# Gated mix of attention and a gated linear unit: alternating periods, value sums copied by ACT, maxima turned by DVE

## The chip, the cores and the metric

The kernel runs on one NeuronCore of a Trainium2 chip. The metric is the device time of one execution in microseconds (us). PE is the matmul engine TensorE (PEld its weight loads), DVE the vector engine VectorE, ACT the scalar engine ScalarE, POOL GpSimd, and SP the engine whose queue issues nearly all DMAs. PE writes its results to PSUM, which has eight banks of 128 x 512 f32.

## The reference

```python
S, D, H, Dh, F = 2048, 512, 32, 16, 1792
g = sigmoid((x * gate_w).sum(-1, keepdims=True))
q, k, v = split(x @ wqkv)                       # 32 heads of 16
a = softmax(q k^T / sqrt(Dh)) v  @ wo           # per head over 2048 keys
b = (sigmoid(x @ w_gate) * (x @ w_up)) @ w_down
return g * a + (1 - g) * b
```

## The kernel before, in words

All matmuls but those of the values take operands that are split into a high and a low part (`split`), so that a product becomes three. Attention goes over 16 pairs of heads. The first head of a pair lies in partitions 0 to 63 (the lower half of PE), the second in 64 to 127 (the upper half): matmuls of the two halves run beside each other on PE if they are issued next to each other.

For each head the row maxima of the scores are found first (`sm_step`: a 128 x 512 score matmul, L250, and a DVE reduce, L252). The maxima of eight query tiles (half of a head's rows, called a half here) are gathered in `stat`, reduced to one row (L256), turned by a PE transpose (`put_max`, L262), copied by ACT (L264), split by POOL (L95, L96) and written by DMA (L270) into two more rows of the query operand QS, so that the second pass (`st_part`: matmul L453, exponential on ACT L455) gets scores with the maximum taken off. Its exponentials `p` go with `v` into the value matmuls (`values`, L468: 16 matmuls of 17 columns, four of which run beside each other). Their result is copied out of PSUM (L473 on ACT in the first four periods, L475 on DVE later) and added up by POOL (`later`, L485).

The main loop has 256 periods (`for k in range(NPER)`). The order within a period is written out by hand in a string, STEADY: `t0` and `t1` are second-pass matmuls of the lower and the upper head, `m0` and `m1` those for maxima, `d0` and `d1` the lower and upper half of a matmul of the dense products (q, k, gate and up projections, one bank, `dn`, for all). A number after the colon names one of seven banks. A period has four t0, four t1, four m0, four m1, six d0 and six d1, then the value matmuls: 14 pairs of half matmuls, 16 banks given to scores and one (`SUMS`) to values. A dense product (`Sum`, "run" below) takes 24 halves, that is two periods, and `turn` lets POOL pass a token from its last upper half matmul to its first lower one, since both write one bank. This happens within every period (between d1 and d0) and at its end. Maxima run 20 to 22 steps ahead of the second pass (FIRST, LEAD). The last eight periods use LAST, without maxima and with half of the dense work. Before the loop come the projections of the first pair and of v with the first maxima (`first_max`), after it the remaining dense products, the gated product, w_down and wo.

The names in rows: `st`, `sm` and `dn` are banks, `qs`/`ks` the operands, `p` exponentials, `stat` maxima, `part`/`sum` value sums, `gu` and `qk` dense results, `pv_d`, `gu_d`, `q_d`, `k_d` tensors in DRAM.

Of the kernel before, what the change touches and what calls it, by code (L numbers as in the profile page):

```python
# [1 line left out]

# [22 lines left out]
P = 128  # L25
# [19 lines left out]
def gated_mix(ctx, tc, x, xT, wqkv, wo, w_gate, w_up, w_down, gate_w, ident, out):  # L45
    nc = tc.nc
# [24 lines left out]
    pv_d = dram.tile([2, NPAIR, P, 512], F32, name="pv_d")  # L71
    rec_d = dram.tile([P, 512], F32, name="rec_d")

    warm = keep.tile([P, 1], F32, name="warm")
    dve.memset(warm, 0.0)
    z = warm.bitcast(F32R)
    for _ in range(WARM):
        pe.matmul(banks[2], z.to_broadcast([P, P]), z.to_broadcast([P, 512]), start=True, stop=True)
    idt = keep.tile([P, P], F32, name="idt")
    den = keep.tile([P, 512], F32, name="den")  # L80
# [16 lines left out]

    def raw_weights(src, shape, name):
        raw = keep.tile(shape, F32, name=name + "r", tag="wr", bufs=2)
        sp.dma_start(raw, src)  # L100
        return raw, shape, name

    def raw_cols(src, c0, name):
        return raw_weights(src[:, c0:c0 + P].rearrange("(k p) f -> p k f", p=P), [P, KT, P], name)

# [71 lines left out]
    def load_x(c):  # L177
        raw = mid(f"x{c}")
        cols = slice(c * 512, (c + 1) * 512)
        for k in range(KT):  # L180
            sp.dma_start(raw[:, k, :], xT[k * P:(k + 1) * P, cols])
        return raw
# [36 lines left out]

    act.activation(g1[:, :1], warm, AF.Exp)  # L220
    ones = v.rearrange("p t (h c) -> p t h c", c=VW)[:, :, :, DH]
    pool.memset(ones, 1.0)
    w_q = split_weights(raw_cols(wqkv, 0, "q0"), act, dve)
# [5 lines left out]
    w_k = split_weights(raw_cols(wqkv, D, "k0"), act, dve)  # L229
    xr.update((c, load_x(c)) for c in range(1, NC))  # L230

# [5 lines left out]
    def sm_step(j):  # L237

        p, s = divmod(j, 32)
        qt, kh = divmod(s, 2)  # L240
        qs, ks = QS[p % 2], KS[p % 2]
        half = (p, qt // 8)
        if half not in stat:
            stat[half] = keep.tile([P, 2, 8, 4], F32, name=f"stat{p}_{qt // 8}", tag="stat", bufs=2)
            count[half] = 0

        def one(b, i):
            r, g = 64 * b, 2 * kh + i
            t = bankm()
            pe.matmul(t, qs[r:r + KM, qt * P:(qt + 1) * P], ks[r:r + KM, g * 512:(g + 1) * 512],  # L250
                      start=True, stop=True)
            dve.tensor_reduce(stat[half][:, b, qt % 8, g:g + 1], t, axis=AX.X, op=ALU.max)  # L252
            count[half] += 1
            if count[half] == 64:
                m = keep.tile([P, 2, 8], F32, name=f"m{p}_{qt // 8}", tag="m", bufs=2)
                dve.tensor_reduce(m, stat.pop(half), axis=AX.X, op=ALU.max)  # L256
                mrow[half] = m
        return one

    def put_max(half, t):  # L260
        p, i = half
        pe.transpose(t[:16, :P], mrow.pop(half).rearrange("p a b -> p (a b)"), idt)  # L262
        raw = keep.tile([16, P], F32, name=f"mr{p}_{i}", tag="mr", bufs=2)
        act.activation(raw, t[:16, :P], AF.Copy)  # L264
        hl = keep.tile([16, 2, P], F32R, name=f"mhl{p}_{i}", tag="mhl", bufs=2)
        split(hl[:, 0, :], hl[:, 1, :], raw, pool, pool)
        for b in range(2):
            for a in range(2):
                r = 64 * b + 3 * DH + a
                sp.dma_start(QS[p % 2][r:r + 1, i * 1024:(i + 1) * 1024].bitcast(F32),  # L270
                             hl[8 * b:8 * b + 8, a, :].bitcast(F32))


    wd = []

    def filling():
        jobs = [("qk", c) for c in range(1, D // P)] + [("gu", f) for f in range(NF)] + [("down", 0)]

        def raws(kind, n):
            if kind == "qk":  # L280
                return [raw_cols(wqkv, n * P, f"q{n}"), raw_cols(wqkv, D + n * P, f"k{n}")]
            if kind == "gu":
                return [raw_cols(w_gate, n * P, f"g{n}"), raw_cols(w_up, n * P, f"u{n}")]
# [25 lines left out]

    first = [(j, i) for j in [*range(0, 16, 2), *range(1, 16, 2), *range(16, FIRST)] for i in range(2)]  # L310

    def first_max():
        if first:
            j, i = first.pop(0)
            one = sm_step(j)
            one(0, i)
            one(1, i)

    for c in range(NC):
        if c + 1 < NC:  # L320
            split_x(c + 1, xr.pop(c + 1))
        if c == 0:
            wv_r = mid("wv_r")
            sp.dma_start(wv_r, wqkv[:, 2 * D:].rearrange("(k p) f -> p k f", p=P))
# [10 lines left out]
    sp.dma_start(idt, ident)  # L335
    sp.dma_start(gwb, gate_w.unsqueeze(0).to_broadcast([P, D]))
# [19 lines left out]
    for t in range(2, NS, 2):  # L356
        two = [Sum(bankv(), tokens(t + a)) for a in range(2)]
        for g in (LOW, UP):
            first_max()
            for m in range(3 * KT):  # L360
                two[0].half(g)
                two[1].half(1 - g)
                if m in (5, 11):
                    first_max()
                if (0, 0) in mrow and g == UP:
                    put_max((0, 0), bankm())
            if g == LOW:
# [92 lines left out]
    def values(k):  # L460
# [10 lines left out]
        def put(e):  # L471
            if k < LEAD - FIRST << 1:
                act.activation(e, o, AF.Copy)  # L473
            else:
                dve.tensor_copy(e, o)  # L475
        if half not in sums:
# [12 lines left out]
    def mx(b):  # L489
        for j in range(FIRST, NSTEP):  # L490
            one = sm_step(j)
# [10 lines left out]

    spot = []

    def emit(order, **parts):

        for word in order.split():
            if word == "turn":
                turn(run)
                work(1)  # L510
            else:
                kind, _, b = word.partition(":")
                spot[:] = [seven[int(b)]] if b else []
                next(parts[kind], None)

    STEADY = ("t0:2 d1 m0:4 d1 t0:1 d1 m0:3 d1 t0:6 d1 d1 turn m0:0 t0:2 t1:4 "
              "d0 m1:1 t1:5 d0 d0 m1:3 t1:6 d0 d0 m1:0 d0 t1:2 m1:4 m0:1")
    SUMS, MAXIMA = 5, 0
    LAST = "t0 d1 t0 d1 t0 d1 turn t0 t1 t1 d0 t1 d0 t1 d0"

# [7 lines left out]
    for _ in ahead:  # L528
        pass
    bank = bankm = lambda: spot[0]  # L530
    for k in range(NPER):
        n = 2 * k
        if n + LEAD == NSTEP:
            bank = bank7
# [5 lines left out]
        if n % 32 == 0 and n // 32 + 1 < NPAIR:  # L540
            load_pair(n // 32 + 1)
        ahead = [half for half in mrow]
# [3 lines left out]
        emit(STEADY if k < NPER - TAIL else LAST, **parts)  # L546
        if k == NPER - 1:
# [6 lines left out]
        if k == NPER - 1:  # L554
            break
        spot[:] = [seven[SUMS]]
        values(k)
        for half in ahead:
            put_max(half, seven[MAXIMA])
        if n == NSTEP - 16:  # L560
# [118 lines left out]


# [18 lines left out]
```

## Time and profile before

| | us |
|---|---|
| median of 3 runs | 1771.85 (1771.55 to 1772.71) |
| span of the profiled execution | 1769.9 |
| PE busy, of the span | 1756.4 |
| DVE busy | 1565.4 |
| ACT busy | 1209.9 |
| POOL busy | 477.7 |

The profile is of one execution. Its span is the time from its first to its last instruction; the time of that execution itself, with what lies around it, is not among the runs listed, whose median stands 1.95 us above the span. Matmuls overlap in the records, so busy time of PE is not a measure of its pace: the starts of matmuls are. In the timeline a row gives start, length, engine, line, operation, out<-in and how many are merged.

### The profile page before, as it was taken

The numbers are of one execution on the slowest core, as the hardware profiler recorded it, in microseconds if no ns is written. First come the engines' busy times: TensorE is split into PE (matmuls) and PEld (weight loads), VectorE is DVE, ScalarE is ACT, GpSimd is POOL, SyncE is SP. The second block draws the span as 40 slices with busy tenths as digits, with TensorE's granted clock in tenths as the row PEclk, the third lists the DMA queues.
The fourth block names the chain that finished last, engine by engine and source line by source line (L and its number), as shares of the span: only waits on it lengthen the run. The fifth ranks groups of instructions, "written<-read, shape, count | busy, mean of one in ns | idle before, by whom it ended". The sixth has DMA issues, their size and how long they took to land.

```text
span 1769.9 us, 33479 instructions
## 1 busy us (share of the span) xinstructions
PE 1756.4 (99%) x12708; PEld 1109.5 (63%) x12708; DVE 1565.4 (88%) x2503; ACT 1209.9 (68%) x2343; POOL 477.7 (27%) x435
## 2 busy tenths in 40 slices
PE   9999999999999999999999999999999999999999
PEld 7756566666555555555666666666565665588887
DVE  6989999999999999999999999999999997456543
ACT  4177777777777777777777777777777777844221
POOL 1124343432132222222222222222222222342110
PEclk9999999999999999999999999999999999999999
DMA  9312323241312131313031212112121212367762
GB/s 247 83 37 67 79 67 91 67 102 43 79 55 67 44 84 49 84 49 84 31 71 39 65 45 60 50 53 51 50 49 51 58 46 75 114 226 249 239 190 71
DMA packets 91633, 148.78 MB, mean 84 GB/s; under 512 B 10128, under 2 KB 37904, under 8 KB 88592
## 3 DMA queue, kind: packets, MB, share of 16 engines
q1 hardware_dynamic: 91472, 146.64, 29.9%
q8 instruction: 100, 1.64, 0.4%
q14 instruction: 61, 0.50, 0.1%
HBM read 87.10 MB, written 58.98 MB: 83 GB/s over the span
## 4 chain that ended last, share of the span: by engine, by line
PE 96%; DVE 3%; DMA 1%; issue 0%; ACT 0%; SPq 0%; DVEq 0%; POOL 0%
PE st L468 26%; PE dn L144 25%; PE sm L453 11%; PE sm L661 7%; PE sm L250 6%; PE st L250 5%; PE st L453 5%; PE st L131 4%; PE dn L661 2%; DVE stat L252 1%; PE st L144 1%; PE st L570 1%; PE sm L570 1%; PE sm L468 1%; DVE part L475 1%; DVE xn L439 1%
## 5 line engine op out<-in xcount | busy, mean ns | idle before, releaser
L252 DVE TENSOR_REDUCE stat<-sm 128x1 f32<-128x512 f32 x1554 | 971.5, 681 | 9.8 <-PE sm L250 6.3
L455 ACT ACTIVATE p<-sm 128x512 f32<-128x512 f32 x1029 | 608.5, 625 | 303.5 <-PE dn L144 196.6
L250 PE MATMUL sm<-ks,qs 48*128 48x512 f32 x1554 | 632.1, 415 | 0.1
L455 ACT ACTIVATE p<-st 128x512 f32<-128x512 f32 x1019 | 564.6, 635 | 14.3 <-PE st L453 10.7
L485 POOL TENSOR_TENSOR sum<-sum,part 128x512 f32<-128x512 f32 x224 | 289.3, 1292 | 868.9 <-PE sm L453 685.6
L468 PE MATMUL st<-p,v 128*17 128x512 f32 x4000 | 478.1, 595 | 0.0
L453 PE MATMUL st<-qs,ks 64*128 64x512 f32 x1019 | 422.8, 419 | 7.9 <-DVE stat L252 5.9
L453 PE MATMUL sm<-qs,ks 64*128 64x512 f32 x1029 | 425.2, 419 | 0.0
L252 DVE TENSOR_REDUCE stat<-st 128x1 f32<-128x512 f32 x494 | 336.5, 682 | 2.5 <-PE st L250 0.9
L453 PEld LDWEIGHTS sm<-qs,ks 64*128 64x128 f32 x1029 | 190.0, 186 | 209.5 <-issue 105.5
L250 PEld LDWEIGHTS sm<-ks,qs 48*128 48x128 f32 x1554 | 283.7, 184 | 29.4 <-DVE stat L252 10.1
L468 PEld LDWEIGHTS st<-p,v 128*17 128x17 f32 x4000 | 92.7, 96 | 216.9 <-issue 155.8
L453 PEld LDWEIGHTS st<-qs,ks 64*128 64x128 f32 x1019 | 188.6, 186 | 47.6 <-DVE stat L252 16.6
L250 PE MATMUL st<-ks,qs 48*128 48x512 f32 x494 | 195.0, 395 | 0.5 <-ACT p L455 0.5
L475 DVE COPY part<-st 128x512 f32<-128x512 f32 x216 | 149.3, 691 | 40.0 <-PE st L468 38.0
L250 PEld LDWEIGHTS st<-ks,qs 48*128 48x128 f32 x494 | 91.4, 185 | 21.2 <-ACT p L455 1.1
L417 DVE TENSOR_TENSOR gul<-gul 128x1024 f32<-128x1024 f32 (+1 forms) x30 | 46.1, 1542 | 35.9 <-ACT gul L416 33.7
L661 PE MATMUL sm<-wd_h,hl 128*128 128x512 f32 x208 | 68.3, 395 | 0.0
L306 ACT ACTIVATE gu<-dn 128x512 f32<-128x512 f32 x98 | 66.5, 679 | 0.0
L93 ACT ACTIVATE hl<-gul 128x1024 fp32r<-128x1024 f32 (+1 forms) x30 | 29.9, 997 | 40.1 <-PE sm L661 26.0
L96 POOL TENSOR_TENSOR ol<-ot,oh 128x1024 fp32r<-128x1024 f32 x8 | 19.3, 2412 | 113.8 <-ACT oh L93 113.8
L93 ACT ACTIVATE oh<-ot 128x1024 fp32r<-128x1024 f32 x8 | 8.5, 1061 | 57.0 <-DVE ot L619 51.7
(459 smaller groups left out, 2978.4 us busy)
## 6 DMA issues: line engine op xcount, KB each, us to landing
gu_d<-gu SPq DMA_DIRECT2D x112, 256.0 KB
gul<-gu_d SPq DMA_DIRECT2D x56, 512.0 KB
qs<-q_d SPq DMA_DIRECT2D x90, 128.0 KB
ks<-k_d SPq DMA_DIRECT2D x90, 128.0 KB
pv_d<-sum SPq DMA_DIRECT2D x32, 256.0 KB
q_d<-qe SPq DMA_DIRECT2D x12, 512.0 KB
k_d<-qe SPq DMA_DIRECT2D x12, 512.0 KB
x<-in_xT_dram SPq DMA_DIRECT2D x16, 256.0 KB
```

The costliest lines, as they stand in the source:

```text
L131: pe.matmul(o, a, b, start=(i == 0), stop=(i == len(ops) - 1))
L144: mm = pe.matmul(self.o, a[rows], b[rows], start=(self.n == 0), stop=(self.n == 2 * len(self.ops) - 1))
L250: pe.matmul(t, qs[r:r + KM, qt * P:(qt + 1) * P], ks[r:r + KM, g * 512:(g + 1) * 512], start=True, stop=True)
L252: dve.tensor_reduce(stat[half][:, b, qt % 8, g:g + 1], t, axis=AX.X, op=ALU.max)
L306: leave = lambda e, o: act.activation(e, o, AF.Copy)
L417: dve.tensor_tensor(gu[:, 1, a], gu[:, 0, a], gu[:, 1, a], ALU.mult)
L453: pe.matmul(o, ks[r:r + KR, (kt + a) * P:(kt + a + 1) * P], qs[r:r + KR, q0:q0 + 512], start=True, stop=True)
L455: act.activation(pt[:, 2 * a + c, :], o, AF.Exp, scale=DH ** -0.5)
L468: pe.matmul(o[32 * c:32 * c + VW, :], v[:, 2 * k % 16 + a, h * VW:(h + 1) * VW], pts[c // 2][:, 2 * a + c % 2, :], start=(a == 0), stop=(a ...
L475: dve.tensor_copy(e, o)
L485: pool.tensor_tensor(s, s, e, ALU.add)
L661: pe.matmul(down[t], a, b, start=(f == 0 and m == 0), stop=(f == NF - 2 and m == 5))
```

## The change

Periods come in twos. An even period takes all twelve upper halves of a dense run (d1) beside eight t0 (of this period and the next), six m0 and two m1; the odd one takes its twelve lower halves beside eight t1, six m1 and two m0. So `turn` is called once for a run, between two periods, and not within one. Which bank a matmul or a value sum gets is told by REUSE: an entry says how many allocations earlier that bank was given. One entry stands for each of the 17 allocations of an even and of an odd period. ACT makes every value copy. The maxima of each head have a tile and a final reduce of their own (L261); POOL splits them (L96, L97), DVE turns them in 32 x 32 blocks (L275), a DMA stores them to DRAM (`m_d`, L276), and two DMAs load them into QS (L280). Upper heads run two steps further ahead (`FIRST + 2 * b`). LAST stands for ten periods. Inputs are laid out on the host so that a weight tile is contiguous, and the first two weights are loaded from ACT's queue.

```diff
-LEAD = 22
-TAIL = 8
+TAIL = FIRST // 2
+DELAY = 2
...
+    q0 = raw_cols(wqk, 0, "q0", act)
+    k0 = raw_cols(wqk, 4, "k0", act)
     xr = {0: load_x(0)}
+    w_q = split_weights(q0, act, dve)
...
+                stat[half] = keep.tile([P, 8, 4], F32, name=f"stat{p}_{qt // 8}_{b}", tag="stat", bufs=4)
...
-            if count[half] == 64:
-                m = keep.tile([P, 2, 8], F32, name=f"m{p}_{qt // 8}", tag="m", bufs=2)
+            if count[half] == 32:
+                m = keep.tile([P, 8], F32, name=f"m{p}_{qt // 8}_{b}", tag="m", bufs=2)
                 dve.tensor_reduce(m, stat.pop(half), axis=AX.X, op=ALU.max)
...
-    def put_max(half, t):
...
+    def split_max(half):
+        hl = square()
+        split(hl[:, 0, :8].bitcast(F32R), hl[:, 1, :8].bitcast(F32R), mrow.pop(half), pool, pool)
+        left = iter(range(DELAY))
+        turning.append((lambda: next(left, None) is None, half, hl))
+
+    def turn_max():
+        _, half, hl = turning.pop(0)
+        p, i, b = half
+        mt = keep.tile([P, 32], F32, name=f"mt{p}_{i}_{b}", tag="mt", bufs=2)
+        dve.transpose(mt, hl.rearrange("p a t -> p (a t)"))
+        sp.dma_start(m_d[p, i, b], mt)
+        rows = m_d[p, i, b].rearrange("(g a t) j -> a t g j", g=4, a=2)
+        for a in range(2):
+            r = 64 * b + 3 * DH + a
+            sp.dma_start(QS[p % 2][r:r + 1, i * 1024:(i + 1) * 1024].bitcast(F32).rearrange(
+                "o (t g j) -> o t g j", g=4, j=32), rows[a, :8].unsqueeze(0))
...
-    first = [(j, i) for j in [*range(0, 16, 2), *range(1, 16, 2), *range(16, FIRST)] for i in range(2)]
+    first = [(j, i) for j in [*range(0, 16, 2), *range(1, 16, 2), *range(16, FIRST + 1)] for i in range(2)]
...
         def put(e):
-            if k < LEAD - FIRST << 1:
-                act.activation(e, o, AF.Copy)
-            else:
-                dve.tensor_copy(e, o)
+            act.activation(e, o, AF.Copy)
...
-        for j in range(FIRST, NSTEP):
+        for j in range(FIRST + 2 * b, NSTEP):
...
+    def place():
+        b = given[-REUSE[count_given[0] % len(REUSE)]]
+        count_given[0] += 1
+        given.append(b)
+        return b
...
-    STEADY = ("t0:2 d1 m0:4 d1 t0:1 d1 m0:3 d1 t0:6 d1 d1 turn m0:0 t0:2 t1:4 "
...
+    STEADY = ("t0 m1 d1 m0 t0 d1 d1 m0 t0 d1 t0 d1 d1 m0 d1 work m0 t0 d1 t0 d1 d1 t0 m1 t0 d1 m0 d1 m0",
...
+    REUSE = (7, 5, 8, 6, 9, 7, 7, 6, 8, 6, 8, 6, 8, 7, 7, 6, 8,
+             7, 7, 7, 7, 7, 7, 7, 6, 8, 7, 7, 7, 7, 6, 8, 6, 8)
-    LAST = "t0 d1 t0 d1 t0 d1 turn t0 t1 t1 d0 t1 d0 t1 d0"
+    LAST = ["t0 d1 t0 d1 t0 d1 d1 turn work t0 t1 t1 d0 t1 d0 t1 d0 d0"] * (TAIL - 4) + [
+        "t0 d1 t0 d1 t0 d1 turn work t0 t1 t1 d0 t1 d0 t1 d0"] * 4
...
-        parts["t0"], parts["t1"] = st_part(k, 0), st_part(k + 1, 1) if k + 1 < NPER else iter(())
-        if k < LEAD - FIRST << 1:
-            emit("m0:0 m1:6", **parts)
+        elif k % 2 == 0:
+            parts["t0"] = chain(st_part(k, 0), st_part(k + 1, 0))
+        else:
+            parts["t1"] = chain(st_part(k, 1), st_part(k + 1, 1))
```

How the order moves is seen best at three places of the steady loop. PE first, the last rows ahead of the values of a period and the values' first. Before:

```order
L453 MATMUL sm_71<-qs_106,ks_107 128x512
L250 MATMUL st_65<-ks_107,qs_106 128x512
L250 MATMUL sm_70<-ks_107,qs_106 128x512
L468 MATMUL st_66<-p_1_9043,v 17x512 x2
L468 MATMUL st_66<-p_0_9079,v 17x512 x2
```

and in the changed kernel, allocations 13 to 17 of an even period:

```order
L255 MATMUL st_65<-ks_107,qs_106 128x512
L468 MATMUL sm_70<-qs_106,ks_107 128x512
L145 MATMUL dn<-xl,g5h 128x512
L255 MATMUL st_66<-ks_107,qs_106 128x512
L145 MATMUL dn<-xh,g5l 128x512
L255 MATMUL sm_69<-ks_107,qs_106 128x512
L483 MATMUL st_67<-p_1_9094,v 17x512 x2
```

Dense halves now stand between scores up to the end, and the values' bank moves from `st_66` to the one that REUSE names, here that of allocation 9. Next ACT, the exponentials (L455, now L470) around a period's end, with a dense copy (`gu`). Before:

```order
L455 ACTIVATE p_1_9611<-st_67 128x512
L455 ACTIVATE p_1_9611<-sm_71 128x512
L306 ACTIVATE gu_1_1_9636<-dn 128x512
L455 ACTIVATE p_0_9653<-sm_71 128x512
L455 ACTIVATE p_0_9653<-sm_70 128x512
```

Changed:

```order
L470 ACTIVATE p_1_8833<-sm_70 128x512
L470 ACTIVATE p_1_8833<-sm_71 128x512
L317 ACTIVATE gu_2_1_8853<-dn 128x512
L487 ACTIVATE part_8868<-sm_69 128x512
L470 ACTIVATE p_0_8871<-st_65 128x512
L470 ACTIVATE p_0_8871<-sm_71 128x512
```

The value copy (L487) stands ahead of the next period's exponentials. Last SP, the rows around the maxima of a half. Before, four loads follow each other straight from POOL's tile `mhl`:

```order
L299 DMA gu_d<-gu_3_0_8997 128x512
L270 DMA qs_106<-mhl_0_9013 1x8x128 x4
L218 DMA qs_108<-q_d 16x2048 x3
L299 DMA gu_d<-gu_3_1_9127 128x512
L218 DMA qs_108<-q_d 16x2048 x3
```

Changed:

```order
L276 DMA m_d<-mt_0_1_7954 128x32
L310 DMA gu_d<-gu_3_0_7974 128x512
L280 DMA qs_108<-m_d 1x32x32 x2
L276 DMA m_d<-mt_0_0_7996 128x32
L218 DMA qs_106<-q_d 16x2048
L280 DMA qs_108<-m_d 1x32x32 x2
L310 DMA gu_d<-gu_3_1_8098 128x512
```

Each head's maxima take a store and two loads that wait for it, with one other DMA between the store and the loads.

More of the change, by code (lines that the diff above doesn't have):

```diff
@@ L1 @@
 from contextlib import ExitStack
+from itertools import chain
 import numpy as np
@@ L39, with gated_mix @@
 NPER = NSTEP // 2
[L40 removed]
+TAIL = FIRST // 2
+DELAY = 2
 LOW, UP = 0, 1
 @with_exitstack
[L45 removed]
+def gated_mix(ctx, tc, x, xc, wqk, wv, wo, w_gu, w_down, gate_w, out):
     nc = tc.nc
@@ L72, in gated_mix @@
     rec_d = dram.tile([P, 512], F32, name="rec_d")
+    m_d = dram.tile([NPAIR, 2, 2, P, 32], F32, name="m_d")
     warm = keep.tile([P, 1], F32, name="warm")
@@ L220, in gated_mix @@
     act.activation(g1[:, :1], warm, AF.Exp)
+    square = ring(keep, 2, [P, 2, 16], "mhl")
+    for _ in range(2):
+        pool.memset(square(), 0.0)
     ones = v.rearrange("p t (h c) -> p t h c", c=VW)[:, :, :, DH]
     pool.memset(ones, 1.0)
-    w_q = split_weights(raw_cols(wqkv, 0, "q0"), act, dve)
+    q0 = raw_cols(wqk, 0, "q0", act)
+    k0 = raw_cols(wqk, 4, "k0", act)
     xr = {0: load_x(0)}
+    w_q = split_weights(q0, act, dve)
     for b in range(2):
@@ L241, in sm_step @@
         qs, ks = QS[p % 2], KS[p % 2]
[L242 to L245, printed above, removed]
         def one(b, i):
+            half = (p, qt // 8, b)
+            if half not in stat:
+                stat[half] = keep.tile([P, 8, 4], F32, name=f"stat{p}_{qt // 8}_{b}", tag="stat", bufs=4)
+                count[half] = 0
             r, g = 64 * b, 2 * kh + i
@@ L258, in sm_step @@
         return one
-    def put_max(half, t):
[L261 to L271, printed above, removed]
+    def split_max(half):
[14 more added lines that the diff above has]
+                "o (t g j) -> o t g j", g=4, j=32), rows[a, :8].unsqueeze(0))
+    turning = []
     wd = []
@@ L314, in first_max @@
             j, i = first.pop(0)
-            one = sm_step(j)
-            one(0, i)
-            one(1, i)
+            if j < FIRST:
+                sm_step(j)(0, i)
+                sm_step(j)(1, i)
+            else:
+                for j in range(FIRST, FIRST + 2):
+                    sm_step(j)(1, i)
     for c in range(NC):
@@ L364, in gated_mix @@
                     first_max()
-                if (0, 0) in mrow and g == UP:
-                    put_max((0, 0), bankm())
+                if turning and turning[0][0]():
+                    turn_max()
+                for half in list(mrow):
+                    split_max(half)
             if g == LOW:
@@ L501, in dense @@
             yield
-    spot = []
+    given = [*seven, *seven]
+    count_given = [0]
+    def place():
[3 more added lines that the diff above has]
+        return b
     def emit(order, **parts):
@@ L509, in emit @@
                 turn(run)
+            elif word == "work":
                 work(1)
             else:
[L512 to L519 removed]
+                next(parts[word], None)
+                if word[0] == "m":
+                    if turning and turning[0][0]():
+                        turn_max()
+                    for half in list(mrow):
+                        split_max(half)
+    STEADY = ("t0 m1 d1 m0 t0 d1 d1 m0 t0 d1 t0 d1 d1 m0 d1 work m0 t0 d1 t0 d1 d1 t0 m1 t0 d1 m0 d1 m0",
+              "t1 m0 t1 d0 d0 m1 t1 d0 d0 m1 d0 m1 t1 d0 work m1 d0 t1 d0 d0 t1 m1 m0 t1 d0 d0 t1 d0 m1")
+    REUSE = (7, 5, 8, 6, 9, 7, 7, 6, 8, 6, 8, 6, 8, 7, 7, 6, 8,
+             7, 7, 7, 7, 7, 7, 7, 6, 8, 7, 7, 7, 7, 6, 8, 6, 8)
+    LAST = ["t0 d1 t0 d1 t0 d1 d1 turn work t0 t1 t1 d0 t1 d0 t1 d0 d0"] * (TAIL - 4) + [
+        "t0 d1 t0 d1 t0 d1 turn work t0 t1 t1 d0 t1 d0 t1 d0"] * 4
     parts = {"m0": mx(0), "m1": mx(1), "d0": dense(LOW), "d1": dense(UP)}
@@ L529, in gated_mix @@
         pass
-    bank = bankm = lambda: spot[0]
+    bank = bankm = place
     for k in range(NPER):
         n = 2 * k
-        if n + LEAD == NSTEP:
+        if n + FIRST == NSTEP:
             bank = bank7
@@ L541, in gated_mix @@
             load_pair(n // 32 + 1)
-        ahead = [half for half in mrow]
-        parts["t0"], parts["t1"] = st_part(k, 0), st_part(k + 1, 1) if k + 1 < NPER else iter(())
-        if k < LEAD - FIRST << 1:
-            emit("m0:0 m1:6", **parts)
-        emit(STEADY if k < NPER - TAIL else LAST, **parts)
+        if k >= NPER - TAIL:
+            parts["t0"], parts["t1"] = st_part(k, 0), st_part(k + 1, 1) if k + 1 < NPER else iter(())
+        elif k % 2 == 0:
+            parts["t0"] = chain(st_part(k, 0), st_part(k + 1, 0))
+        else:
+            parts["t1"] = chain(st_part(k, 1), st_part(k + 1, 1))
+        if k >= NPER - TAIL and turning:
+            turn_max()
+        emit(STEADY[k % 2] if k < NPER - TAIL else LAST[k - NPER], **parts)
         if k == NPER - 1:
@@ L678, in gated_mix, with by_tiles @@
         late_next()
+def by_tiles(w):
+    w = np.asarray(w)
+    return w.reshape(KT, P, w.shape[1] // P, P).transpose(2, 1, 0, 3)
 def kernel(A_x, A_wqkv, A_wo, B_x, B_w_gate, B_w_up, B_w_down, gate_w):
```

34 lines of the change are left out of this document (15 added, 19 removed).

## The prediction

> **What bounds the kernel now.** I read the page first, its span and its engines.
>
> ```profile
> span 1769.9 us, 33479 instructions
> PE 1756.4 (99%) x12708; PEld 1109.5 (63%) x12708; DVE 1565.4 (88%) x2503; ACT 1209.9 (68%) x2343; POOL 477.7 (27%) x435
> ```
>
> PE seems to be the bound. So I looked at two stretches of exactly 16 periods of the main loop. The columns are the stretch, its length, and the busy time of PE, PEld, DVE, ACT and POOL.
>
> ```profile
> 1013.20:1103.65 90.45, 90.45 (x707) 54.97 (x706) 88.03 (x147) 68.84 (x139) 23.21 (x22) 1.00 0.21 54
> 646.20:739.10 92.90, 91.75 (x707) 53.75 (x706) 90.51 (x155) 69.30 (x139) 23.16 (x22) 1.00 0.25 63
> ```
>
> A period takes 5.65 us in the first and 5.81 in the second, where DVE also does eight logits. PE and DVE (97%) both look full, so one period decides, by its timelines (start, length, engine, line). PE's:
>
> ```profile
> 1103.71 1.91 PE L468 MATMUL st<-p,v 128*17 128x512 f32 x16
> 1105.55 0.49 PE L453 MATMUL sm<-qs,ks 64*128 64x512 f32 x1
> ...
> 1105.89 0.39 PE L250 MATMUL st<-ks,qs 48*128 48x512 f32 x1
> ...
> 1106.12 0.39 PE L453 MATMUL sm<-qs,ks 64*128 64x512 f32 x1
> ...
> 1108.88 0.50 PE L250 MATMUL sm<-ks,qs 48*128 48x512 f32 x1
> 1109.31 1.91 PE L468 MATMUL st<-p,v 128*17 128x512 f32 x16
> 1111.15 0.49 PE L453 MATMUL sm<-qs,ks 64*128 64x512 f32 x1
> ```
>
> and DVE's:
>
> ```profile
> 1105.75 0.69 DVE L475 COPY sum<-st 128x512 f32<-128x512 f32 x1
> 1106.36 0.68 DVE L252 TENSOR_REDUCE stat<-st 128x1 f32<-128x512 f32 x1
> 1106.95 3.07 DVE L252 TENSOR_REDUCE stat<-sm 128x1 f32<-128x512 f32 x5
> 1109.94 0.68 DVE L252 TENSOR_REDUCE stat<-st 128x1 f32<-128x512 f32 x1
> 1110.54 0.68 DVE L252 TENSOR_REDUCE stat<-sm 128x1 f32<-128x512 f32 x1
> 1111.39 0.69 DVE L475 COPY part<-st 128x512 f32<-128x512 f32 x1 [0.17 <-PE st L468]
> ```
>
> DVE is without a gap but the one before the copy. It starts a reduce every (1109.94 - 1106.95)/5 = 0.598 us; eight make 4.78, the copy holds it for 0.61 (1105.75 to 1106.36), and the wait for the value matmuls costs 1111.39 - 1110.54 - 0.60 = 0.25. Together 5.64: this is the period. PE is not full: a matmul is shown as 0.39 long, but pairs start 0.23 apart (1105.89 to 1106.12). [...]
>
> Of PE's period, 1.84 us are values (1103.71 to 1105.55) and 3.76 the pairs (1105.55 to 1109.31). Fourteen unhindered pairs need 0.34 to the second (1105.55 to 1105.89), 12 x 0.23, and 0.32 from the last to the values, as in the tail:
>
> ```profile
> 1515.38 0.39 PE L144 MATMUL dn<-xh,g12l 64*128 64x512 f32 x1
> 1515.70 1.95 PE L468 MATMUL st<-p,v 128*17 128x512 f32 x16
> ...
> 1519.57 2.00 PE L468 MATMUL st<-p,v 128*17 128x512 f32 x16
> ```
>
> That is 3.43, so PE's own floor is 5.27 us.
>
> **The copy moves to ACT.** DVE loses 0.61 + 0.25 a period and needs 4.78. ACT gains a copy. Its own pace:
>
> ```profile
> 1108.01 1.61 ACT L455 ACTIVATE p<-st 128x512 f32<-128x512 f32 x3
> 1109.44 0.67 ACT L455 ACTIVATE p<-sm 128x512 f32<-128x512 f32 x1
> ```
>
> An exponential each (1109.44 - 1108.01)/3 = 0.477; eight are 3.82, half a copy of a dense sum adds 0.24, and the new copy, which has the same shape, is taken at 0.50 (between 0.48, an exponential's, and the 0.64 below): 4.6 of 5.6 us, so ACT does not become the bound. Its new wait for the values stands ahead of the next eight exponentials, and through their banks ahead of PE. What the copy delays is read in the first periods of the loop, where ACT already does it:
>
> ```profile
> 94.89 1.91 PE L468 MATMUL st<-p,v 128*17 128x512 f32 x16
> ...
> 96.74 0.50 PE L250 MATMUL sm<-ks,qs 48*128 48x512 f32 x1
> ...
> 96.87 0.60 ACT L473 ACTIVATE sum<-st 128x512 f32<-128x512 f32 x1 [1.21 <-PE st L468]
> ...
> 97.28 0.69 DVE L252 TENSOR_REDUCE stat<-sm 128x1 f32<-128x512 f32 x1 [0.47 <-PE st L250]
> ...
> 97.51 1.08 ACT L455 ACTIVATE p<-sm 128x512 f32<-128x512 f32 x2
> ```
>
> Count from the first pair of a period (96.74 here). The copy starts at 0.13 and DVE's first reduce at 0.54. The exponential behind the copy, here 0.64 later, belongs to PE's third row and waited for it; with a score as first word it can start at 0.13 + 0.50 = 0.63.
>
> **The new limit: banks.** A matmul can only take a bank that its reader has left. PE follows 0.06 us after the reader's end (the first of two reduces that began at 104.42 ended at 105.10):
>
> ```profile
> 104.42 1.28 DVE L252 TENSOR_REDUCE stat<-st 128x1 f32<-128x512 f32 x2
> ...
> 105.16 0.50 PE L453 MATMUL st<-qs,ks 64*128 64x512 f32 x1 [0.43 <-DVE stat L252]
> ```
>
> For ACT I take the same 0.06. Reduce n then ends at 0.54 + 0.598(n-1) + 0.68, exponential n at 0.63 + 0.477(n-1) + 0.66 (its length: 1.61 - 2 x 0.477). I walked both new periods with REUSE in hand. Both give the same. Allocations 8 to 13 find their banks free (8 wants one at 1.49, free at 1.28). Allocation 14 wants 2.66 and gets the bank of exponential 4 at 2.78; allocation 15 wants 3.01 and gets that of reduce 4 at 3.07; allocation 16 follows at 3.30; the values, allocation 17, are ready at 3.62 and get the bank of reduce 5 at 0.54 + 4 x 0.598 + 0.68 + 0.06 = 3.67. With 1.84 for the values: 5.51 us. A stalled matmul lengthens the step behind it (1108.88 above: 0.50 instead of 0.39, and 0.43 instead of 0.32 to the values). With that at 14 (2.78 + 0.34 = 3.12, then 3.35) and at 16 (0.43) the values start at 3.78: 5.62. I take 5.53, near the lower end, since the next matmul is covered by the other half of PE. The in-period turn goes: the one left each two periods waits beside the values.
>
> **Maxima and logits.** The reduce to one row:
>
> ```profile
> L256 DVE TENSOR_REDUCE m<-stat x32: 220/220/222, 76.3 to 1490.4; 128x16 f32<-128x64 f32 x32
> ```
>
> It comes 64 instead of 32 times, with a DVE transpose each. The transpose has no row; it lies between DVE's smallest operation here (0.08, the logit's below) and a large reduce (0.68), and is nearest in size to this one. One of each, per eight periods, stands ahead of a fifth reduce: 2 x (0.22 - 0.08 overlap) / 8 = 0.04 a period (0.02 to 0.15 by the ends). PE's transpose (0.2 us each eighth period) and ACT's copy of it go. A logit costs DVE 0.60:
>
> ```profile
> 706.60 0.68 DVE L439 CUSTOM_DVE_ANT_0 xn<-xn,gwb 128x512 f32<-128x512 f32 x1
> 707.20 0.08 DVE L439 DVE_READ_ACCUMULATOR2_ANT logit<- 128x1 f32 x1
> ```
>
> It now fits the gap between reduce 8 (0.54 + 8 x 0.598 = 5.32) and the next period's first (5.53 + 0.54), so it is free; if that gap closed, 16 x 0.6 = 10 us would be back.
>
> **Sum.** The loop's first values start at 94.89 (above), those of period 245 and 254 here:
>
> ```profile
> 1493.61 1.91 PE L468 MATMUL sm<-p,v 128*17 128x512 f32 x16
> 1531.35 1.99 PE L468 MATMUL st<-p,v 128*17 128x512 f32 x16
> ```
>
> 245 periods took 1398.7 us, 5.71 each. At 5.53 + 0.04 = 5.57 they take 1364.7: -34.0. The nine of the tail took 37.7, 4.2 each. Their last ones run at ACT's pace (3.87, 1515.70 to 1519.57, for eight exponentials); with the copy 3.82 + 0.50 + 0.1 = 4.4, so 39.6: +1.9. The head: four extra maxima matmuls leave the first periods and four others join the value projection: 0. The first weights, now on ACT's queue, start behind the table load and x half a microsecond earlier; PE is busy with warm-up matmuls until 7.1 us:
>
> ```profile
> 0.74 0.44 SPq L100 DMA_DIRECT2D q0r<-in_wqkv_dram  x1
> ...
> 0.92 6.22 PE L78 MATMUL st<-warm 128*128 128x512 f32 x20 [0.92 <-DVE warm L75]
> ...
> 3.83 0.63 ACT L93 ACTIVATE q0h<-q0r 128x512 fp32r<-128x512 f32 x1 [1.60 <-DMA q0r<-in_wqkv_dram]
> ```
>
> so 0 within +-1; contiguous weight loads hide behind whole runs. The span falls by 32 to 1738; the runs' median stands 1.95 above the profiled span: 1740 us. Under 0.2% (3.5 us) counts as no change.
>
> **Rivals.** *PE's floor:* if no bank were late, 5.31 a period, 245 x 0.40 = 98 saved, 1676. Reduce 5 speaks against it, unless the first reduce starts earlier than 0.54. Chance 0.07.
> *More stalls:* every late bank costs a restart, or the transpose holds DVE while POOL is in one of its additions: 5.62 to 5.67, 1752 to 1764. Chance 0.18.
> *PE is the bound, as its 99% says:* only the 32 transposes go, 32 x 0.2 = 6, and the tail gives 2 back: 1768, the edge of no change. The pitch of 0.23 speaks against it. Chance 0.06.
> *Slower, the maximum rows arrive late:* POOL's split, DVE's transpose, a store to DRAM and two loads now follow each other. Rows: 0.28 and 0.45 on POOL, 0.64 per issue, and 2.65 from issue to use for 256 KB (1.18 to 3.83 above).
>
> ```profile
> L95 POOL CAST mhl<-mr x32: 279/280/283, 77.8 to 1496.2; 16x128 fp32r<-16x128 f32 x32
> L96 POOL TENSOR_TENSOR mhl<-mr,mhl x32: 446/450/460, 78.2 to 1496.5; 16x128 fp32r<-16x128 f32 x32
> L270 SPq DMA_DIRECT2D qs<-mhl x128: 634/635/1518, 78.1 to 1498.6; - x128
> ```
>
> On SP a store of a dense sum stands between them, whose data are ready by then, and before half of the chains a load of q_d, which waits for scores of the period before. Behind the blocked SP are only stores of four-fold buffered sums and loads of weights for later runs.
>
> For a lower head the transpose stands behind the second reduce of period 8h-2, at about 2.2; store 0.64 + 2.65, loads 2 x 0.64 + 2.65: 9.4, and the scores need the rows at 2 x 5.53 = 11.1. So 1.7 us are left, nothing if a DMA takes 3.5, and from 4.1 each, with 31 halves late by a microsecond, the gain is gone: 1775 and more. Chance 0.09. [...]
>
> **How the numbers follow.** Forecast (1730 to 1750) 0.60, the rivals as given. Faster: 0.60 + 0.18 + 0.07 = 0.85; same 0.06; slower 0.09. The range leaves out the floor and the late rows. Below it allows 10 us more than the forecast's own end, a first reduce 0.04 us earlier in each period; above it goes to the case without a gain: 1720 to 1768.
>
> **What would show it.** Values to values 5.5 to 5.6 us; DVE with idle time before the first reduce, waiting for PE; PE's waits naming DVE and ACT ahead of scores and values; an ACT copy at 0.13; logit periods as long as others; score matmuls waiting for no DMA. I am wrong if DVE is still without gaps, if a PE wait names m_d, or if periods differ much between even and odd.

## The result, and the profile after

The changed kernel takes 1758.58 us (median of four runs, 1757.89 to 1758.72) against 1771.93 for the kernel before beside it: a ratio of 0.9921 (95% interval 0.9907 to 0.9935), 13.4 us less. The forecast was 32 us less; the time lies in its range, the size does not agree. The page of the changed kernel:

```profile
span 1756.2 us, 33183 instructions
PE 1749.5 (100%) x12676; PEld 1060.2 (60%) x12676; DVE 1422.0 (81%) x2346; ACT 1321.8 (75%) x2564; POOL 478.1 (27%) x501
```

DVE went from 88% to 81%, ACT from 68% to 75%: the copies have moved. But this is what two stretches of 16 periods became, the plain one and the one with logits (columns as in the prediction):

```profile
1000.36:1090.71 90.35, 90.35 (x705) 50.95 (x704) 79.08 (x137) 76.16 (x153) 23.27 (x26) 1.00 0.23 55
639.00:729.35 90.35, 90.35 (x705) 50.96 (x704) 81.49 (x145) 76.14 (x153) 23.28 (x26) 1.00 0.28 67
```

The plain stretch took 90.45 us before and takes 90.35: though DVE does 9 us less in it, it gained next to nothing. The one with logits fell from 92.90 to the same 90.35. There are four of these, so 10.2 us of the gain lie in them: 9.8 are logits that now cost no time, 4 x (92.90 - 90.45), and the rest is the plain 0.10 of each. The boundaries of the loop (first values, those of period 245 and of period 254):

```profile
96.82 0.73 PE L483 MATMUL sm<-p,v 128*17 128x512 f32 x4
...
1479.95 0.62 PE L483 MATMUL sm<-p,v 128*17 128x512 f32 x4
...
1519.37 0.62 PE L483 MATMUL sm<-p,v 128*17 128x512 f32 x4
```

| part of the span | before | after | difference | forecast |
|---|---|---|---|---|
| up to the first values | 94.89 | 96.82 | +1.9 | 0 |
| 245 periods | 1398.7 | 1383.1 | -15.6 | -34.0 |
| nine of the tail | 37.7 | 39.4 | +1.7 | +1.9 |
| from the values of period 254 to the end | 238.6 | 236.8 | -1.7 | none made |

Of the 15.6 us, 10.2 are the four stretches with logits and 2.7 the first four periods (25.2 to 22.5 us). Four single long periods of before (one of 6.23, three of 6.0) have gone, which is 1.7, and the remaining 1.0 is spread over all other periods.

Where a plain period ends is seen in one (PE, then its weight loads, ACT and DVE; first pair at 1013.43, dense halves mostly left out):

```profile
1013.43 0.49 PE L255 MATMUL st<-ks,qs 48*128 48x512 f32 x1
...
1015.87 0.56 PE L255 MATMUL sm<-ks,qs 48*128 48x512 f32 x2
1016.22 0.49 PE L468 MATMUL st<-qs,ks 64*128 64x512 f32 x1
...
1016.55 0.47 PE L468 MATMUL st<-qs,ks 64*128 64x512 f32 x1
1016.56 0.39 PE L145 MATMUL dn<-xl,u7h 64*128 64x512 f32 x1
1016.79 0.39 PE L145 MATMUL dn<-xh,u7l 64*128 64x512 f32 x1
1016.87 0.40 PE L255 MATMUL sm<-ks,qs 48*128 48x512 f32 x1
1017.19 1.91 PE L483 MATMUL st<-p,v 128*17 128x512 f32 x16
1019.03 0.49 PE L468 MATMUL sm<-qs,ks 64*128 64x512 f32 x1
```

```profile
1016.22 0.18 PEld L468 LDWEIGHTS st<-qs,ks 64*128 64x128 f32 x1
...
1016.33 0.19 PEld L145 LDWEIGHTS dn<-xl,u7h 64*128 64x128 f32 x1
1016.53 0.18 PEld L468 LDWEIGHTS st<-qs,ks 64*128 64x128 f32 x1
...
1016.71 0.18 PEld L255 LDWEIGHTS sm<-ks,qs 48*128 48x128 f32 x1
```

```profile
1013.61 0.60 ACT L487 ACTIVATE part<-st 128x512 f32<-128x512 f32 x1 [1.09 <-issue]
...
1015.53 0.63 ACT L470 ACTIVATE p<-st 128x512 f32<-128x512 f32 x1
```

```profile
1013.99 0.69 DVE L257 TENSOR_REDUCE stat<-st 128x1 f32<-128x512 f32 x1 [0.73 <-PE st L468]
...
1015.80 1.28 DVE L257 TENSOR_REDUCE stat<-st 128x1 f32<-128x512 f32 x2
```

DVE waits 0.73 us ahead of its first reduce: it no longer sets the period. ACT's fourth exponential ends at 1015.53 + 0.63 = 1016.16, and allocation 14 starts at 1016.22, 2.79 after the first pair. The forecast had 2.78. What follows is not as forecast: the next scores come 0.33, 0.32 and the values again 0.32 later (1016.55, 1016.87, 1017.19), so the values start at 3.76 and the period is 5.60. The rows of PEld say why. A weight load that nothing holds starts here up to 0.23 ahead of its matmul: the dense load at 1016.33 belongs to the matmul at 1016.56. That of allocation 14 starts together with its matmul, so its time is not hidden, and the next score comes 0.33 later. The step at the start of a period, 0.34 in the prediction, is as long, and there too load and matmul start together (both at 1013.43 here). The load of allocation 15 then waits for a bank in its turn: the fourth reduce, the first of the two at 1015.80, ends at 1016.48, and the load starts at 1016.53, only 0.02 ahead of its matmul. The step behind it is 0.32. So each late bank holds the weight load and lengthens the next step by some 0.1. The dense half beside it has a step of 0.23 again (1016.56 to 1016.79): it does not make up for the other half, it only runs ahead. These rows show that a wait for a bank takes the lead of 0.23 from a weight load: allocation 14 has 0.00 left of it and allocation 15 has 0.02.

### The profile page after: what moved, and what is told of

It reads as the page before. It is cut to its first block, busy times and chain, and to the rows that moved or that the text cites. A ratio compares the mean times of both kernels' runs of the same rounds, so it can differ in the third digit from the quotient of the medians.

```text
span 1756.2 us, 33183 instructions
## 1 busy us (share of the span) xinstructions
PE 1749.5 (100%) x12676; PEld 1060.2 (60%) x12676; DVE 1422.0 (81%) x2346; ACT 1321.8 (75%) x2564; POOL 478.1 (27%) x501
## 4 chain that ended last, share of the span: by engine, by line
PE 99%; DVE 0%; ACT 0%; issue 0%
PE dn L145 19%; PE sm L483 16%; PE sm L468 12%; PE st L483 11%; PE sm L255 10%; PE st L468 9%; PE sm L688 7%; PE st L255 7%; PE st L132 4%; PE dn L688 2%; PE st L145 1%; PE sm L597 1%; PE st L597 1%; PE st L80 0%; DVE stat L257 0%; ACT p L470 0%
## 5 line engine op out<-in xcount | busy, mean ns | idle before, releaser
L257 DVE TENSOR_REDUCE stat<-sm 128x1 f32<-128x512 f32 x1205 | 774.2, 680 | 100.3 <-PE sm L255 87.4
L470 ACT ACTIVATE p<-sm 128x512 f32<-128x512 f32 x1167 | 666.9, 652 | 0.1
L257 DVE TENSOR_REDUCE stat<-st 128x1 f32<-128x512 f32 x843 | 552.0, 679 | 70.9 <-PE st L255 61.9
L470 ACT ACTIVATE p<-st 128x512 f32<-128x512 f32 x881 | 522.2, 652 | 9.2 <-PE st L468 8.6
L255 PE MATMUL sm<-ks,qs 48*128 48x512 f32 x1205 | 463.7, 419 | 0.2 <-DVE stat L257 0.2
L468 PE MATMUL st<-qs,ks 64*128 64x512 f32 x881 | 351.6, 425 | 1.5 <-ACT v L361 1.4
L255 PE MATMUL st<-ks,qs 48*128 48x512 f32 x843 | 341.8, 419 | 0.0
L483 PE MATMUL sm<-p,v 128*17 128x512 f32 x2384 | 285.1, 595 | 0.0
L255 PEld LDWEIGHTS sm<-ks,qs 48*128 48x128 f32 x1205 | 218.3, 185 | 38.1 <-DVE stat L257 7.8
L483 PE MATMUL st<-p,v 128*17 128x512 f32 x1712 | 204.6, 595 | 0.0
L255 PEld LDWEIGHTS st<-ks,qs 48*128 48x128 f32 x843 | 155.4, 185 | 25.0 <-DVE stat L257 3.0
L487 ACT ACTIVATE part<-sm 128x512 f32<-128x512 f32 x132 | 81.1, 614 | 107.8 <-issue 92.7
L487 ACT ACTIVATE part<-st 128x512 f32<-128x512 f32 x92 | 56.2, 611 | 77.7 <-issue 62.9
L96 POOL CAST mhl<-m 128x8 fp32r<-128x8 f32 x64 | 12.1, 189 | 272.7 <-DVE m L261 272.7
```

What stands on the lines that cost most here:

```text
L257: dve.tensor_reduce(stat[half][:, qt % 8, g:g + 1], t, axis=AX.X, op=ALU.max)
L468: pe.matmul(o, ks[r:r + KR, (kt + a) * P:(kt + a + 1) * P], qs[r:r + KR, q0:q0 + 512], start=True, stop=True)
L470: act.activation(pt[:, 2 * a + c, :], o, AF.Exp, scale=DH ** -0.5)
L483: pe.matmul(o[32 * c:32 * c + VW, :], v[:, 2 * k % 16 + a, h * VW:(h + 1) * VW], pts[c // 2][:, 2 * a + c % 2, :], start=(a == 0), stop=(a ...
```

## The experiments

The theory: two chains free the banks (DVE's reduces, ACT's copy and exponentials), both come late at the end of a period, and each late bank costs PE the weight load besides. First each chain was shortened, alone and together.

**short_reduce**: `tensor_reduce(..., t[:, :384], ...)`, maxima over 384 of 512 columns.

> The changed kernel, but each reduce for a maximum reads 384 of a bank's 512 columns (the last quarter of the scores is left out of the maximum). A plain period of the changed kernel takes 5.61 us where 5.53 was forecast. Theory (both sides): allocation 14 waits for ACT's fourth exponential (2.74 + 0.05 after the first pair), restarts cost 0.33 + 0.32 + 0.32 to the values, and DVE's fourth reduce (3.05 + 0.05) is only just not late; so a faster DVE alone leaves a plain period at 5.58 to 5.61, and only the two longer periods of eight shrink: 1745 to 1758 us. Rival 1 (the forecast's path: the fifth reduce decides): 4 x 0.12 + 0.12 less, plain periods of 5.1 to 5.3, under 1700 us. Rival 2 (PE itself needs 5.6): 5.61, 1750 to 1758 us.

1729.53 us, ratio 0.976 (0.9745 to 0.9774). The plain period fell from 5.61 to 5.55, 0.03 below the theory's lower 5.58, which is 7 us over 245 periods, and the total lies 16 us below the lower end. The theory had the fourth reduce as only just not late. For the matmul it was not, but it was for the weight load, and that lengthened the step to allocation 16. Behind allocation 14, still late by ACT, the step is 0.34 as before (1001.31 to 1001.65 in one period), though the load behind it waits for no bank (1001.41). The periods with maxima became as short as the others, as written. The first values came at 92.8 instead of 96.8, which I had left out: DVE bounds the head too.

**short_copy**: the value copy and POOL's addition over 256 of 512 columns.

> The changed kernel, but ACT's copies into part and POOL's additions take 256 of 512 columns (half of the value sums is left out in seven of eight periods). Theory (both sides): exponential 4 ends 0.2 earlier, allocation 14 is no longer late, but allocation 15 then waits for reduce 4 at 3.10 and restarts from there, so a plain period falls by 0.02 to 0.06 only: 1743 to 1755 us. Rival 1 (fifth reduce): no change, 1758. Rival 2 (PE itself): no change, 1758. A rival to both, ACT alone decides: 0.2 less in 215 periods, 1715 us.

1758.1 us, 0.9919 (0.9905 to 0.9934): no change, 3 us above the theory's range. ACT's exponentials come 0.14 earlier and allocation 14 starts at 2.67, but 15 waits for the fourth reduce and starts at 3.11, as before (3.12), with 0.33 to each of the next two starts. ACT alone is not the limit.

**short_both**: both cuts.

> Both cuts together: reduces over 384 columns, part copies and additions over 256. Theory (both sides): no bank is late any more, a plain period comes near PE's floor, 5.27 to 5.38 us, 1680 to 1710 us, far more than the sum of the two single cuts. Rival 1 (fifth reduce): the same as reduces over 384 alone. Rival 2 (PE itself): 5.6, 1750 to 1758. ACT alone: the same as the short copy alone.

1698.44 us, 0.9583 (0.9569 to 0.9598), in the range of the theory: 5.41 a plain period, 0.20 less, where the single cuts gave 0.06 and 0.00. It is 0.03 above the 5.38 of the theory, for one bank is still late. That one also shows how little lateness costs a weight load. The bank of the next score was free at some 1003.58 (its exponential is the third of these four); its partner in the other half, a score for maxima, started at 1003.57:

```profile
1001.95 2.06 ACT L470 ACTIVATE p<-st 128x512 f32<-128x512 f32 x4
```

```profile
1003.36 0.40 PE L468 MATMUL st<-qs,ks 64*128 64x512 f32 x1
1003.57 0.40 PE L255 MATMUL sm<-ks,qs 48*128 48x512 f32 x1
1003.59 0.48 PE L468 MATMUL st<-qs,ks 64*128 64x512 f32 x1
...
1003.91 0.40 PE L255 MATMUL sm<-ks,qs 48*128 48x512 f32 x1
```

```profile
1003.13 0.18 PEld L468 LDWEIGHTS st<-qs,ks 64*128 64x128 f32 x1
...
1003.57 0.18 PEld L468 LDWEIGHTS st<-qs,ks 64*128 64x128 f32 x1
...
1003.68 0.19 PEld L255 LDWEIGHTS sm<-ks,qs 48*128 48x128 f32 x1
```

The matmul is 0.02 late at most, and the next score of its half still comes 0.32 instead of 0.23 behind it (1003.59 to 1003.91), though the load of that one, at 1003.68, waits for no bank. The load of the score before had started at 1003.13, 0.23 ahead of its matmul. So a bank counts as late when the load wants to start, here some 0.2 before the matmul.

**doubles_last**: the pair with two banks is put last; nothing else.

```diff
-"... d1 d1 t0 m1 t0 d1 m0 d1 m0",   "... d0 t1 m1 m0 t1 d0 d0 t1 d0 m1"
+"... d1 d1 t0 d1 t0 d1 m0 m0 m1",   "... d0 t1 m1 d0 t1 d0 d0 t1 m0 m1"
```

> The changed kernel with the same words in another order: the pair in which both halves take a bank (allocations 13 and 14 in even, 12 and 13 in odd periods) is moved to the end of each period, so allocations 14 and 15 are wanted 0.23 later. Nothing is left out. Theory (both sides): allocation 14 wants 2.89 and finds exponential 4's bank at 2.79, 15 wants 3.12 and finds reduce 4's at 3.10, 16 waits until 3.28, the values start at 3.70 instead of 3.77: 5.55 us a period, 1743 to 1750 us. Rival 1 (fifth reduce): values at 3.70 too, but from 3.77 that would be its own bound already, so no change, 1757 to 1759. Rival 2 (PE itself): no change, 1757 to 1759.

1744.94 us, 0.9843 (0.9826 to 0.9859), as expected. Allocations 14 and 15 now start at 2.93 and 3.14, within 0.04 of where they are wanted (2.89 and 3.12), and the plain period is 5.55. The same work in another order of pairs gains 13.6 us on the changed kernel, as much as the change itself gained.

Then the change was taken apart.

**before_act**: the kernel before with `act.activation(e, o, AF.Copy)` for every period.

> The kernel before, its order kept, with all value copies on ACT: the copy alone. Theory (DVE's 0.61 us copy and the 0.25 us behind it made the old period; after that the late banks do): the plain period falls from 5.65 to 5.58-5.63, the eight-logit stretches no longer stick out, 1745-1758 us, most of the change's gain without its order. Rival 1 (the new order is what helps, the copy only moves the wait to ACT): 1765-1775. Rival 2 (the order costs and hides a larger gain of the copy): below 1740.

1760.36 us, 0.9936 (0.9921 to 0.9951), 2 us above the range. The stretches that were 90.45 and 92.90:

```profile
1000.36:1090.63 90.27, 90.27 (x708) 52.67 (x707) 78.47 (x132) 76.27 (x155) 23.20 (x22) 1.00 0.21 54
639.29:729.53 90.24, 90.24 (x709) 52.82 (x707) 80.89 (x140) 76.28 (x155) 23.23 (x22) 1.00 0.24 64
```

The copy alone gives nearly the gain of the whole change: logits hidden, the plain period 5.63. The new order by itself adds nothing to it (90.35 against 90.27). Its tail is 40.7 us, 1.3 longer than that of the changed kernel.

**after_dve**: the changed kernel with `dve.tensor_copy(e, o)`, the order alone.

> The changed kernel with all value copies on DVE again: the order alone. Theory: the copy starts about 0.13 after the first pair and holds DVE 0.61, so the first reduce starts at 0.75, the fifth ends at 0.75 + 4 x 0.598 + 0.68 = 3.82 and the values get its bank at 3.87: a period of 5.71, more where maxima or logits lie, 1775-1800 us. Rival (the order alone brings part of the gain): 1760-1770.

1818.38 us, 1.026 (1.0245 to 1.0275), 46 us slower than before, worse than the range. The rows of PE, then of DVE:

```profile
1047.41 0.50 PE L468 MATMUL sm<-qs,ks 64*128 64x512 f32 x1
...
1050.69 0.50 PE L468 MATMUL sm<-qs,ks 64*128 64x512 f32 x1
...
1051.03 0.40 PE L255 MATMUL st<-ks,qs 48*128 48x512 f32 x1
1051.36 1.91 PE L483 MATMUL sm<-p,v 128*17 128x512 f32 x16
```

```profile
1047.55 0.69 DVE L487 COPY sum<-sm 128x512 f32<-128x512 f32 x1 [0.30 <-PE sm L483]
1048.16 0.68 DVE L257 TENSOR_REDUCE stat<-sm 128x1 f32<-128x512 f32 x1
```

The copy starts 0.14 after the first pair, the first reduce at 0.75, as written; the fifth ends at 3.82. But the values start at 3.95 instead of 3.87, and not for the fifth reduce. The fourth, ending at 0.75 + 3 x 0.598 + 0.68 = 3.22, holds allocation 15 until 3.28 (1050.69); then come two steps of 0.34 and 0.33, as in the changed kernel. The expectation had left these out. So plain odd periods take 5.78, even ones 5.85. The logits cost 0.6 each again. So the new order needs the copy on ACT, and the copy does not need the order.

**same_lead**: `range(FIRST + 2 * b, NSTEP)` becomes `range(FIRST, NSTEP)`, and the four extra maxima matmuls of the head go. This tries the rival of late maximum rows.

> The changed kernel with upper heads no further ahead than lower ones (20 steps), which also takes four maxima matmuls out of the head. Theory: the store is waited for 1.45 us and not 3.3 as forecast, but upper rows are now written a period later and needed 7.5 us after the transpose behind both heads' DMAs on SP: they come late by 0 to 2.5 us a half, 31 halves, so 1757-1830 us, with a PE wait for m_d's rows if late; the first values come 1.5 to 2.5 us earlier (95 us instead of 96.8). Rival (the lead is not needed, rows are in time as in the changed kernel): 1755-1758, the head's 2 us alone.

1920.1 us, 1.0834 (1.0817 to 1.0851), far above the range. One period of eight takes 6.9 to 12.7 us, and the one behind it up to 7.3. PE, SP and POOL in one of them (12.2 us):

```profile
1041.06 0.39 SPq L276 DMA_DIRECT2D m_d<-mt  x1
...
1044.72 1.26 POOL L119 TENSOR_TENSOR g7l<-g7r,g7h 128x512 fp32r<-128x512 f32 x1
1046.01 0.34 SPq L101 DMA_DIRECT2D g8r<-in_w_gu_dram  x1
1046.44 1.38 SPq L280 DMA_DIRECT2D qs<-m_d  x2
1049.40 0.76 PE L468 MATMUL sm<-qs,ks 64*128 64x512 f32 x1 [5.41 <-DMA qs<-m_d]
```

On SP the load of a later run's weights (g8r) stands between the store of the rows and their loads. Its buffer is free only when POOL has split the weights before (1045.98), so the loads are issued 5.4 us after the store, and not 1.5 as in the changed kernel (below), behind a transfer that nobody needs yet. Such a load stands there in 12 of the 30 long periods, and these take 12.0 to 12.4 us. Eleven others take 6.9 to 10.0: the rows are late even without it. The first six (10.9 to 12.7) and the last (12.3) have no weight load there either, and I did not follow them. With the lead of two steps the rows of both heads are in time. For such a stall PE then pays a second time:

```profile
1044.00:1049.30 5.30, 0.00 (x0) 0.00 (x0) 1.51 (x3) 0.61 (x2) 1.90 (x3) 0.82 0.19 51
1049.40:1052.20 2.80, 2.80 (x12) 1.94 (x12) 1.15 (x2) 1.81 (x4) 0.00 (x0) 0.50 0.00 0
...
1055.06:1058.00 2.94, 2.94 (x29) 2.46 (x25) 2.37 (x4) 2.74 (x6) 1.29 (x1) 1.00 0.00 0
```

After 5.4 us without a matmul the granted clock is 0.50, and it is 1.00 again from 1055.06 on. The head shortened by 1.0 us (first values at 95.8), less than the 1.5 to 2.5 expected.

**late_maxima** and **best** go on from doubles_last: the upper head's final reduce is held until its period's fifth reduce has been issued; in late_maxima the lower transpose should move behind the eighth, and in best the upper one moves behind the seventh, which makes room for it.

```diff
-            if count[half] == 32:
+            if count[half] == 32:
+                closing.append(half)
+            if closing and (nth[0] > 4 or closing[0][2] == 0):
+                h = closing.pop(0)
                 ...
-        left = iter(range(DELAY))
+        left = iter(range(half[2]))      # late_maxima: DELAY * half[2]
```

> doubles_last with the upper head's final reduce put behind the fifth reduce of its period, and the lower head's transpose behind the eighth instead of behind the second of the next period; nothing is left out. Theory (they cost only because they stand ahead of a fifth reduce, whose bank the values wait for; behind it DVE has 0.7 us to spare): the periods of 5.77 and 5.64 fall to 5.55, 0.31 x 31 = 10 us, 1733-1738 us. Rival (their time on DVE counts wherever they stand, or DVE now waits for POOL's split): 1743-1750.

> late_maxima with the upper transpose behind the seventh reduce, so that the lower one stands behind the eighth and no longer behind the next period's first; nothing is left out. Theory: the one period in eight that was 5.64 falls to 5.55, 0.09 x 31 = 2.8 us below late_maxima: 1734.5-1737.5 us, the fastest so far. Rival (a transpose behind the seventh waits for POOL's split and delays the eighth reduce): 1738-1742.

1738.62 (0.9812, 0.9796 to 0.9829), 0.6 above its range, then 1736.02 (0.9792, 0.9779 to 0.9806), as expected. In late_maxima the 5.77 fell to 5.55, but the lower transpose still stood behind a first reduce, and 5.64 remained; in best that went too, and nearly all of the 245 periods take 5.54 to 5.56. So maxima cost only as far as they stand ahead of a period's fifth reduce. Two chains of best end together:

```profile
999.99 0.50 PE L472 MATMUL st<-qs,ks 64*128 64x512 f32 x1
...
1003.27 0.50 PE L256 MATMUL sm<-ks,qs 48*128 48x512 f32 x1
1003.70 1.91 PE L487 MATMUL st<-p,v 128*17 128x512 f32 x16
```

```profile
1000.56 0.69 DVE L258 TENSOR_REDUCE stat<-st 128x1 f32<-128x512 f32 x1 [0.67 <-PE st L472]
```

```profile
1000.17 0.60 ACT L491 ACTIVATE part<-st 128x512 f32<-128x512 f32 x1 [1.04 <-issue]
...
1002.58 1.62 ACT L474 ACTIVATE p<-sm 128x512 f32<-128x512 f32 x3
```

ACT's fifth exponential (the first of the three at 1002.58, ending at 1003.22) releases the last score at 1003.27, and the values follow 0.43 later. DVE's fifth reduce ends at 1000.56 + 4 x 0.598 + 0.68 = 1003.63, and 0.06 later is 1003.70 as well.

**best_early** moves only ACT's chain (two one-column copies take the value copy's waits for POOL and DVE), **best_short** only DVE's (384 columns), **best_both** both.

```diff
+            act.activation(seen[:, :1], sums[half][:, :1], AF.Copy)
+            act.activation(seen[:, 1:], newest[-4:][0], AF.Copy)
```

> best with two one-column ACT copies, of a sum and of a maximum, ahead of each period's values: they take the value copy's waits for POOL and DVE, so that it waits for PE alone, as in the first periods of the kernel before. The copy should start at 0.13 instead of 0.18 after the first pair. Theory (with the pair of two banks last, the values wait for reduce 5 as well, which does not move): 0 to -3 us against best. Rival (the 0.05 us of the copy's late start is what the forecast missed): -10 to -12 us.

> best with maxima over 384 of 512 columns, all else as it was. Theory 1 (ACT's fifth exponential holds the last score matmul at 3.28, and the values follow 0.43 later, at 3.71): the plain period stays 5.55, only the head gets shorter by 4 us, 1729-1733 us. Theory 2 (the values wait for reduce 5): they come at 3.6 or earlier, 5.44 a period, 1705-1712 us.

> best_early and best_short in one: the value copy waits for PE alone, and maxima are taken over 384 of 512 columns. Each alone left the plain period at 5.55. Theory (two equal limits: ACT's fifth exponential 3.23 + 0.05 + 0.43 to the values, and reduce 5 at 3.65 + 0.06, both 3.71): with both moved the values start at 3.18 + 0.05 + 0.43 = 3.66, 5.50 a period, 0.05 x 245 = 12 us less than best_short where the periods have nothing else in them; with the 4.6 us that the two small copies cost elsewhere 1721-1726 us. Rival (a third limit holds the values at 3.71): 1730-1735.

1740.63 (0.9817, 0.9804 to 0.983), 1730.39 (0.9763, 0.9749 to 0.9776), 1724.38 (0.9724, 0.9708 to 0.974). The copy of best_early does start 0.13 after the first pair, and waits for PE:

```profile
1001.15 0.60 ACT L497 ACTIVATE part<-st 128x512 f32<-128x512 f32 x1 [0.87 <-PE st L493]
```

The plain period stays 5.55 in both single ones and is 5.50 in best_both (first pair and values):

```profile
1005.14 0.50 PE L474 MATMUL st<-qs,ks 64*128 64x512 f32 x1
...
1008.79 1.91 PE L493 MATMUL st<-p,v 128*17 128x512 f32 x16
```

So two limits of the same size are shown, one by one and together. The 0.05 us of ACT's late copy are not what the forecast missed. best_early is 4.6 us slower than best, where 0 to 3 less were expected. The 245 periods take 1361 us in both; the first values come 0.6 later, the tail takes 0.8 longer, and what follows it 3.2. I did not follow why. best beats both kernels with nothing left out.

## Why the prediction was half right

- **What bounds the kernel before: right, but with too little behind it.** DVE without its copy has 0.73 us to spare a period. But the banks held PE at 5.60 to 5.63 in either order, 0.01 to 0.04 below DVE's 5.64.
- **The failed step: "I take 5.53, near the lower end, since the next matmul is covered by the other half of PE".** Measured: 5.60 to 5.61. With the maxima the mean was 5.645 instead of 5.57, and 245 periods times 0.075 are 18 us, all that the 245 periods fell short. The reason for the choice was wrong: a late bank holds the weight load, so the steps behind allocations 14 and 15 take 0.33 and 0.32 instead of 0.23, and the other half runs on without helping. short_both shows this step with the matmul itself 0.02 late at most. The two walks of the prediction ended at 5.51 and 5.62. The second comes near, 3.78 to the values against 3.76, but in part by luck: its steps behind allocation 14 are 0.34, 0.23 and 0.43, the measured ones 0.33, 0.32 and 0.32. The rival "every late bank costs a restart" (5.62 to 5.67, 1752 to 1764) is what came. Nor were allocations 8 to 13 all free in time: in the period above the load of 13 waited until 1015.93 for the third reduce (end 1015.88). That was in the other half than the late scores, and set nothing.
- **The copy's start.** 0.13 was forecast, 0.18 came, and the first reduce at 0.57 instead of 0.54: the copy here waits for DVE, PE and POOL, that in the rows I read for PE and at times POOL. It changed nothing, as DVE's chain ended at about the same time (short_copy and best_early).
- **Maxima: right.** Two periods of eight take 5.83 and 5.70: (0.22 + 0.09) / 8 = 0.04. best shows that the place, not the work, costs it.
- **Logits: right**, 9.8 us hidden, though the "eight logits" of a stretch were eight instructions of DVE, so four logits; the 16 of the whole loop was the right number. **Tail: right**, +1.7 against +1.9.
- **Maximum rows not late: right**, with more room than forecast. The forecast had 0.64 + 2.65 from the store to the first load's issue:

```profile
984.08 0.32 SPq L276 DMA_DIRECT2D m_d<-mt  x1
...
985.55 1.38 SPq L280 DMA_DIRECT2D qs<-m_d  x2
```

  It took 1.47. The rival was real nevertheless: same_lead shows it at 162 us over the changed kernel. What I had put down as harmless "loads of weights for later runs" on the queue is more than half of it: the 12 periods that it held, with those behind them, took some 90 us more than plain ones.
- **The head: wrong by 2 us** (0 forecast, +1.9). same_lead gives 1.0 of it to the four extra maxima matmuls; short_reduce, with first values 4.0 earlier, shows that DVE's pace matters there. The rest, and the 1.7 us gained behind the tail, were not taken apart.

## What to carry to other kernels

Before an engine is relieved, work out when the next limit ends: here it stood 0.03 us behind the one removed, and 0.73 us of a busy engine's time a period bought little but the work that had been on top of it. When a walk over banks gives two ends, look at the weight loads of the stalled matmuls in the trace of before, which decide between them: in the period that the prediction read, a score and its load start together at 1107.09, and the next score comes 0.33 later (1107.42). When two chains end together, shorten both or reorder the consumer: a pair moved by a few places gained as much as the whole change.

## What was not expected of the hardware

- A bank that is 0.02 us late costs the following step some 0.1 (short_both: 0.32 instead of 0.23): the weight load of the score before started 0.23 ahead of its matmul, this one's 0.02 ahead.
- The two halves of PE drift apart: behind a stalled score the next score comes 0.32 to 0.33 later, while the dense half beside it came 0.23 behind the one before (changed kernel, 1016.56 to 1016.79).
- After 5.4 us without matmuls (same_lead) the clock granted to PE was 0.50, and a matmul took 0.62 instead of 0.39, so that this stall cost its period 6.6 (12.2 instead of 5.6).
- A copy that waits for three engines started 0.18 after the first pair, one that waits for PE alone 0.13 (best_early).
